# Left k/v rows on 128 partitions, and a new order of weight conversion, copies and u steps, in an attention with two MLPs

## The chip, the core and the metric

The kernel runs on one core of one Trainium2 chip. The metric is the time of one execution on the device in microseconds (us), the median of a few runs. Five engines work side by side, each through its own instructions in a fixed order: PE (TensorE: matmuls and transposes; its weight loads are shown as PEld), DVE (VectorE), ACT (ScalarE), POOL (GpSimd) and SP (SyncE, which here only issues transfers). Semaphores tie them together. PSUM is the memory PE writes to, SBUF the one that everything else lives in.

## What is computed

The reference, cut to what matters (float32, except that the five weights are float64):

```python
# attention: q, k, v (4, 8, 576, 64), phi (4, 8, 576, 32)
a = softmax(phi, axis=2)                       # over the 576 positions
k_m = einsum('bhsm,bhsd->bhmd', a, k)
v_m = einsum('bhsm,bhsd->bhmd', a, v)
attn = softmax(q @ k_m.transpose(0, 1, 3, 2) / 8)
x = (attn @ v_m), heads merged                 # (2304, 512)
# first MLP: w_a, w_b (512, 1536), w_out (1536, 512)
x = ((x @ w_a) * (x @ w_b)) @ w_out
# second MLP: w_in (512, 2048), w_out (2048, 512), elu between
out = elu(x @ w_in) @ w_out
```

## The kernel before

**Attention, lines 293 to 482 and the loop after line 530.** It runs over four batches, called b here (i in the loop). The eight heads of a batch lie as two halves u, in each of which four heads times 32 memory slots fill 128 partitions. For each batch: `a_max` (DVE), `a_exp` (ACT) and `a_end` (DVE) make the softmax of phi over the positions; `stage_aT` transposes it with PE and ACT copies it to the tile a; `stage_kv` sums k (n = 0) and v (n = 1) over the positions into pk, four times a batch, each with 16 matmuls over four blocks of 128 positions from kv_t and four over the 64 positions that are left, from left_t; `stage_m`, `stage_turn`, `stage_kT` and `stage_vT` scale and place the sums; `stage_scores` makes the scores (sc and, for the 64 positions left, sl); `stage_softmax` (DVE) takes the row maximum off, `stage_exp` (ACT) exponentiates, `stage_norm` (DVE) divides by the sums, and `stage_xT` transposes the result and splits it into xhi (ACT) and xlo (DVE). The row softmax of batch i is finished while batch i+1 runs.

**Weights.** They come as 64-bit words, a unit of 128x512 of them (512 KB) in a tile raw, of which there are three. A unit is turned into float32 parts: two ACT instructions (`magnitude` makes a, `low_word` makes lw) and seven slots of `piece`, six of them with a DVE instruction (about 3.2 us of DVE in a row). `fill(n)` does the next n slots at the place where it is called. Units are numbered in the order of use: ab(0,0), ab(0,1), ab(1,0), ab(1,1), o1(0), ab(2,0) and so on. SP loads three of them among the attention's inputs (("unit",) in the list seq, which `more_loads` works off), POOL the others, one when a conversion reaches slot 3.

**First MLP.** Since x is attn times v_m, `step_u(f, p)` multiplies a column block f of w_a and w_b with v_m of two batches into u_ps; ACT copies it to u's hi part, and a deferred DVE instruction makes the lo part. `steps_ab(f, b)` then multiplies u with xhi and xlo, two PSUM tiles (ab_ps) of 12 matmuls each, and forms a*b (a_sb, gh, gl); `steps_o1` multiplies that with w_out (o_ps). `step` sets the order inside one such step by a string: PE's work, then by ORDER "0f1a2" deferred work of kind 0, the fill, deferred work of kind 1, the evacuation a of the PSUM tile, deferred work of kind 2 (the usual kind). The list `order` sets the order of the steps. `pstile` hands out PSUM tiles in turn: two during the attention, four after it, so a tile must be read out before the second or fourth next is written. The second MLP (`step_h`, `steps_o2`) follows, with the same `step`.

Everything stands on each engine in the order in which the code records it.

Of the kernel before, what the change touches and what calls it, by code (L numbers as in the profile page):

```python
# [21 lines left out]
def attention_then_two_mlps(ctx, tc, q, kv, kv_left, phi, w_ab, w_o1, w_i2, w_o2, out):  # L22
# [15 lines left out]
    M = 32  # L38
# [34 lines left out]
    NRAW, NSHORT, NLONG = 3, 4, 4  # L73
# [19 lines left out]
    cu = {}  # L93
    ready = {}
# [52 lines left out]
    def piece():  # L147
# [70 lines left out]
    FILLS, FILLS2 = (0, 7, 7, 7), (0, 0, 0, 0)  # L218
# [59 lines left out]
    ident = p0.tile([P, P], F32, name="ident", bufs=1)  # L278

# [66 lines left out]
    def a_end(b, u):  # L346
        sm = st["sm", b, u]
        nc.vector.tensor_scalar(out=sm, in0=sm, scalar1=1e-9, scalar2=None, op0=ALU.add)
        nc.vector.reciprocal(out=sm, in_=sm)

    def stage_aT(b, us=(0, 1)):
        t = st["phi", b]
        if us[0] == 0:
            st["a", b] = p0.tile([P, 2, NJ + 1, P], F32, tag="a", name="a_t", bufs=1)
        a = st["a", b]
        tp, tl = pstile("tp_a"), pone("tl_a")
# [6 lines left out]
        nc.scalar.activation(  # L363
            out=a[:, c, 0:NJ, :].rearrange("p u j s -> p u (j s)"), in_=tp[:, c], func=AF.Copy
        )
        nc.scalar.activation(
            out=a[0:LEFT, c, NJ, :], in_=tl[0:LEFT, 0:2 * P].rearrange("p (u s) -> p u s", u=2)[:, c], func=AF.Copy
        )
        if us[-1] == 1:
            more_loads("phi")  # L370

    def stage_kv(b, n, u):
# [113 lines left out]
    def step_u(f, p, amount):  # L486
# [22 lines left out]
        step(pe, lambda: nc.scalar.activation(out=hi, in_=src, func=AF.Copy), amount)  # L509
# [3 lines left out]
    with tc.manual_schedule():  # L513
        make_identity(nc, ident)
        pair = p0.tile([P, 2, 2, P // 2], F32, name="pair", bufs=1)
# [10 lines left out]
        nc.gpsimd.memset(edge, 0.0)  # L526
        more_loads()
        for u in range(2):
            a_max(0, u)
            a_exp(0, u)  # L530
            stage_aT(0, (u,))
        for u in range(2):
            a_end(0, u)
        for i in range(B):

            for n in (1, 0):
# [339 lines left out]
```

## Time and profile before

| | |
|---|---|
| median of 3 runs | 816.09 us (814.43 to 816.77) |
| the profiled execution | 816.6 us, of which 814.8 are the span |
| PE busy, matmuls | 790.4 us (97%) |
| DVE busy | 589.4 us (72%) |
| ACT busy | 398.7 us (49%) |
| read and written in DRAM | 52.17 MB, 4.72 MB |

Busy time is that of an engine's instructions; the profile also names what ended the idle time ahead of an instruction. PEclk is the clock granted to TensorE, 1.00 being 2.4 GHz and 0.50 being 1.2 GHz. A matmul "128x288 x4" in a timeline is four in a row, with the time from the first start to the last end.

### The profile page before, as it was taken

The numbers are of one execution on the slowest core, as the hardware profiler recorded it, in microseconds if no ns is written. First come the engines' busy times: TensorE is split into PE (matmuls) and PEld (weight loads), VectorE is DVE, ScalarE is ACT, GpSimd is POOL, SyncE is SP. The second block draws the span as 40 slices with busy tenths as digits, with TensorE's granted clock in tenths as the row PEclk, the third lists the DMA queues.
The fourth block names the chain that finished last, engine by engine and source line by source line (L and its number), as shares of the span: only waits on it lengthen the run. The fifth ranks groups of instructions, "written<-read, shape, count | busy, mean of one in ns | idle before, by whom it ended". The sixth has DMA issues, their size and how long they took to land.

```text
span 814.8 us, 14254 instructions
## 1 busy us (share of the span) xinstructions
PE 790.4 (97%) x6032; PEld 728.1 (89%) x6032; DVE 589.4 (72%) x971; ACT 398.7 (49%) x616; POOL 40.3 (5%) x87
## 2 busy tenths in 40 slices
PE   5889899999999999999999999999999999999998
PEld 3778889999999999999999889988999888999896
DVE  2689797788868884677878644779777787676564
ACT  4365575534443442343468555445655456553350
POOL 2000010000000000000000000000000000000000
PEclk9899999999999999999999999999999999999999
DMA  9971032121212120011001200111111011100006
GB/s 332 363 277 53 27 109 100 52 79 57 75 52 79 55 76 27 27 53 52 1 27 53 78 1 27 51 53 52 50 53 45 35 52 42 37 0 1 1 1 232
DMA packets 16815, 57.79 MB, mean 71 GB/s; under 512 B 1776, under 2 KB 1776, under 8 KB 16752
## 3 DMA queue, kind: packets, MB, share of 16 engines
q0 software_dynamic: 9360, 34.08, 11.9%
q1 hardware_dynamic: 7392, 22.81, 7.8%
q8 instruction: 47, 0.77, 0.4%
q14 instruction: 16, 0.13, 0.1%
HBM read 52.17 MB, written 4.72 MB: 70 GB/s over the span
## 4 chain that ended last, share of the span: by engine, by line
PE 91%; DVE 4%; DMA 2%; ACT 1%; issue 1%; SPq 0%; DVEq 0%
PE o_ps L776 25%; PE h_ps L733 25%; PE o_ps L639 19%; PE ab_ps L597 18%; PE u_ps L500 2%; DMA y<-in_q_dram 2%; PE pk L383 1%; PE sc L425 1%; DMA kv_t<-in_kv_dram 1%; DVE u L510 0%; DVE y L468 0%; DVE ssm L463 0%; DVE y L452 0%; DVE smx L451 0%; DVE gl L608 0%
## 5 line engine op out<-in xcount | busy, mean ns | idle before, releaser
L597 PE MATMUL ab_ps<-xhi,u 128*128 128x288 f32 x768 | 140.4, 300 | 3.0 <-DVE u L510 3.0
L597 PEld LDWEIGHTS ab_ps<-xhi,u 128*128 128x128 f32 x768 | 115.2, 190 | 9.1 <-issue 3.5
L776 PE MATMUL o_ps<-ulh,g2h 128*128 128x512 f32 x288 | 113.7, 395 | 0.0
L776 PE MATMUL o_ps<-ull,g2h 128*128 128x512 f32 x288 | 113.6, 394 | 0.0
L776 PE MATMUL o_ps<-ulh,g2l 128*128 128x512 f32 x288 | 103.0, 395 | 0.0
L751 DVE SCALAR_TENSOR_TENSOR e<-e,th 128x768 f32<-128x768 f32 x48 | 46.0, 959 | 75.2 <-ACT e L748 74.8
L733 PE MATMUL h_ps<-yh,usl 128*128 128x384 f32 x384 | 97.8, 335 | 0.0
L733 PE MATMUL h_ps<-yl,ush 128*128 128x384 f32 x384 | 97.8, 335 | 0.0
L733 PE MATMUL h_ps<-yh,ush 128*128 128x384 f32 x384 | 97.6, 335 | 0.0
L744 ACT ACTIVATE e<-h_ps 128x768 f32<-128x768 f32 x48 | 38.9, 811 | 96.2 <-PE h_ps L733 94.0
L639 PE MATMUL o_ps<-gh,ulh 128*128 128x288 f32 x384 | 82.6, 296 | 1.8 <-DVE u L510 1.6
L597 PE MATMUL ab_ps<-xlo,u 128*128 128x288 f32 x384 | 82.7, 297 | 0.0
L639 PE MATMUL o_ps<-gh,ull 128*128 128x288 f32 x384 | 82.3, 295 | 0.0
L639 PE MATMUL o_ps<-gl,ulh 128*128 128x288 f32 x384 | 82.3, 295 | 0.0
L604 ACT ACTIVATE a_sb<-ab_ps 128x576 f32<-128x576 f32 x48 | 31.2, 651 | 84.6 <-PE ab_ps L597 84.1
L733 PEld LDWEIGHTS h_ps<-yh,ush 128*128 128x128 f32 x384 | 69.5, 188 | 1.3
L606 DVE TENSOR_TENSOR a_sb<-a_sb,ab_ps 128x576 f32<-128x576 f32 x48 | 36.1, 753 | 47.3 <-PE ab_ps L597 46.9
L733 PEld LDWEIGHTS h_ps<-yh,usl 128*128 128x128 f32 x384 | 69.4, 188 | 0.0
L733 PEld LDWEIGHTS h_ps<-yl,ush 128*128 128x128 f32 x384 | 69.3, 188 | 0.0
L776 PEld LDWEIGHTS o_ps<-ulh,g2l 128*128 128x128 f32 x288 | 54.0, 187 | 13.2
L776 PEld LDWEIGHTS o_ps<-ulh,g2h 128*128 128x128 f32 x288 | 54.0, 187 | 12.7
L776 PEld LDWEIGHTS o_ps<-ull,g2h 128*128 128x128 f32 x288 | 54.0, 187 | 12.5
(92 smaller groups left out, 1331.0 us busy)
## 6 DMA issues: line engine op xcount, KB each, us to landing
raw<-in_w_o_dram POOLq DMA_DIRECT2D x28, 512.0 KB, 3.6
raw<-in_w_ab_dram POOLq DMA_DIRECT2D x21, 512.0 KB, 3.6
kv_t<-in_kv_dram SPq DMA_DIRECT2D x16, 512.0 KB, 12.2
raw<-in_w_i_dram POOLq DMA_DIRECT2D x16, 512.0 KB, 3.5
y<-in_q_dram SPq DMA_DIRECT2D x8, 576.0 KB, 12.6
out_dram<-y SPq DMA_DIRECT2D x8, 512.0 KB, 2.9
phi_t<-in_phi_dram SPq DMA_DIRECT2D x3, 576.0 KB, 11.8
raw<-in_w_ab_dram SPq DMA_DIRECT2D x3, 512.0 KB, 12.3
```

The costliest lines, as they stand in the source:

```text
L383: nc.tensor.matmul(pk[M * h:M * h + M, D * u:D * u + D], a[0:P if j < NJ else LEFT, u, j, M * h:M * h + M], rows, start=(j == 0), stop=(j ...
L425: nc.tensor.matmul(sc[:, u, j * P:(j + 1) * P], qs[u][:, t, j * P:(j + 1) * P], kt[:, u, t * P:(t + 1) * P], start=(t == 0), stop=(t == 1))
L500: nc.tensor.matmul(ps[j:j + M, o, k * 256:k * 256 + 256], vt[r, 2 * k + c, 2 * p + o], w[r, c * 256:c * 256 + 256], start=True, stop=True, ...
L597: nc.tensor.matmul(ps[:, h, 0:HS], u[:, kk, w, n * P:n * P + P], x[b][:, kk, h * HS:(h + 1) * HS], start=(kk == 0 and i == 0), stop=(kk == ...
L604: nc.scalar.activation(out=a_sb, in_=ps[:, :, 0:HS], func=AF.Copy)
L606: nc.vector.tensor_tensor(out=a_sb, in0=a_sb, in1=ps[:, :, 0:HS], op=ALU.mult)
L639: nc.tensor.matmul(ps[:, h, 0:HS], w[:, cc], g[:, h * HS:(h + 1) * HS], start=(n == 0 and i == 0), stop=(n == len(fs) - 1 and i == 2),)
L733: nc.tensor.matmul(ps[:, h, 0:HB], w[:, c], x[:, c, h * HB:(h + 1) * HB], start=(c == 0 and i == 0), stop=(c == KC - 1 and i == 2),)
L744: nc.scalar.activation(out=e, in_=ps[:, :, 0:HB], func=AF.Relu, scale=-1.0)
L751: nc.vector.scalar_tensor_tensor(out=e, in0=e, scalar=1.0, in1=th, op0=ALU.add, op1=ALU.mult)
L776: nc.tensor.matmul(ps[:, k, :], g[:, c * P:(c + 1) * P], w, start=(f == fs[0] and i == 0), stop=(f == fs[-1] and i == 2),)
```

## The change

- **Left rows.** The 64 positions left of both halves u are loaded on 128 partitions, row 2s+u, in one tile of half the width (256 KB as before). `a_end(b, 1)` copies phi's last 64 positions interleaved into rest (DVE), one 128x128 transpose takes the place of two, and two ACT copies with a scale of 0 or 1 per partition (parity) make a_left, one for each u with the other's rows zero.
- **Conversion.** Units 0 and 1 are converted ahead of batch 0, unit 2 at the end of batch 1's transposes, unit 3 in batch 2, none in batch 3. SP loads the first seven units: one behind batch 0's phi, one behind its v, one each in batches 1 and 2, three behind the last q. POOL loads none until then. There are six ush tiles where there were four.
- **Order.** `edge` and the load of ACT's table stand at the start. In batch 3, `stage_exp(2)` stands behind both halves of `stage_m`. A u step's evacuation stands last ("012fa"). In the first MLP's list a `tick` stands ahead of `stage_norm(3)`, the fill of two ab steps (four PSUM tiles) moves to the two after `stage_xT(3)`, and u(2,1) stands behind ab(1,3).

SP, at the start, before and then of the change:

```order
L294 DMA phi_t<-in_phi_dram 128x576 x2
L303 DMA left_t<-in_kv_left_dram 64x1024
L308 DMA kv_t<-in_kv_dram 128x1024 x4
L103 DMA raw<-in_w_ab_dram 128x512
L294 DMA phi_t<-in_phi_dram 128x1152 x2
L298 DMA y_77<-in_q_dram 128x1152 x2
```

```order
L303 DMA phi_t<-in_phi_dram 128x576 x2
L104 DMA raw<-in_w_ab_dram 128x512
L312 DMA left_t<-in_kv_left_dram 128x512
L317 DMA kv_t<-in_kv_dram 128x1024 x2
L104 DMA raw<-in_w_ab_dram 128x512
L317 DMA kv_t<-in_kv_dram 128x1024 x2
L303 DMA phi_t<-in_phi_dram 128x1152 x2
L307 DMA y_77<-in_q_dram 128x1152 x2
```

The unit behind kv_t moved to behind phi, and a second one, which POOL loaded at this time, stands among the kv_t loads.

DVE in batch 1, from the end of the conversion to the row softmax of batch 1 (sc), before and then of the change; ssm and y_79 are the sums and the scores of batch 0:

```order
L182 TENSOR_TENSOR lw<-lw,p_489 128x512
L190 TENSOR_TENSOR ush<-a,lw 128x512
L463 TENSOR_REDUCE ssm<-y_79 128x32
L463 TENSOR_REDUCE ssm<-y_79 64x8
L465 TENSOR_SCALAR ssm<-ssm 128x32
L466 RECIPROCAL ssm<-ssm 128x32
L465 TENSOR_SCALAR ssm<-ssm 64x8
L466 RECIPROCAL ssm<-ssm 64x8
L468 TENSOR_TENSOR y_79<-y_79,ssm 128x1024
L468 TENSOR_TENSOR y_79<-y_79,ssm 64x256
L337 TENSOR_REDUCE nm<-phi_t 128x1 x2
L451 TENSOR_REDUCE smx<-sc 128x32
```

```order
L477 TENSOR_TENSOR y_79<-y_79,ssm 128x1024
L477 TENSOR_TENSOR y_79<-y_79,ssm 64x256
L169 TENSOR_SCALAR a<-a 128x512
L172 TENSOR_SCALAR a<-a 128x512
L177 SCALAR_TENSOR_TENSOR a<-raw,a 128x512
L183 TENSOR_SCALAR p_540<-a 128x512
L189 TENSOR_TENSOR lw<-lw,p_540 128x512
L197 TENSOR_TENSOR ush<-a,lw 128x512
L347 TENSOR_REDUCE nm<-phi_t 128x1 x2
L460 TENSOR_REDUCE smx<-sc 128x32
```

The conversion moved from ahead of `stage_norm(0)` to behind it, ahead of batch 1's row maximum.

DVE in the first MLP, around u(0,1), before and then of the change:

```order
L182 TENSOR_TENSOR lw<-lw,p_1070 128x512
L463 TENSOR_REDUCE ssm<-y_79 128x32
L463 TENSOR_REDUCE ssm<-y_79 64x8
L465 TENSOR_SCALAR ssm<-ssm 128x32
L466 RECIPROCAL ssm<-ssm 128x32
L465 TENSOR_SCALAR ssm<-ssm 64x8
L466 RECIPROCAL ssm<-ssm 64x8
L468 TENSOR_TENSOR y_79<-y_79,ssm 128x1024
L468 TENSOR_TENSOR y_79<-y_79,ssm 64x256
L190 TENSOR_TENSOR a<-a,lw 128x512
L608 TENSOR_TENSOR gl<-a_sb,gh 128x576
L510 TENSOR_TENSOR u<-u_ps,u 128x4x256
```

```order
L189 TENSOR_TENSOR lw<-lw,p_1079 128x512
L623 TENSOR_TENSOR gl<-a_sb,gh 128x576
L519 TENSOR_TENSOR u<-u_ps,u 128x4x256
L472 TENSOR_REDUCE ssm<-y_79 128x32
L472 TENSOR_REDUCE ssm<-y_79 64x8
L474 TENSOR_SCALAR ssm<-ssm 128x32
L475 RECIPROCAL ssm<-ssm 128x32
L474 TENSOR_SCALAR ssm<-ssm 64x8
L475 RECIPROCAL ssm<-ssm 64x8
L477 TENSOR_TENSOR y_79<-y_79,ssm 128x1024
L477 TENSOR_TENSOR y_79<-y_79,ssm 64x256
L621 TENSOR_TENSOR a_sb<-a_sb,ab_ps 128x576 x2
```

u's lo part moved from behind `stage_norm(3)` and a conversion step to ahead of them.

The diff, cut to its core:

```diff
-    NRAW, NSHORT, NLONG = 3, 4, 4
+    NRAW, NSHORT, NPAIR, NLONG = 3, 6, 3, 4
...
+    def ahead():
+        n = state["n"]
+        magnitude(n)
+        low_word(n)
...
-            load_unit()
+            if ("unit",) not in seq:
+                load_unit()
...
-        t = pl.tile([P, 2, 2, 2, P], F32, tag="left", name="left_t", bufs=2)
-        nc.sync.dma_start(out=t[0:LEFT], in_=kv_left[b])
+        t = pl.tile([P, 2, 2, P], F32, tag="left", name="left_t", bufs=2)
+        nc.sync.dma_start(out=t, in_=kv_left[b].rearrange("s u n c d -> (s u) n c d"))
...
-    seq = [("phi", 0, (0,)), ("phi", 0, (1,))]
+    seq += [("phi", 0, (0,)), ("phi", 0, (1,)), ("unit",)]
     for b in range(B):
-        seq += [("left", b)] + [("kv", b, n, u) for n in (1, 0) for u in range(2)]
-        seq += [("unit",)] if b < 3 else []
+        seq += [("left", b)] + [("kv", b, 1, u) for u in range(2)] + [("unit",)] * (b == 0)
+        seq += [("kv", b, 0, u) for u in range(2)] + [("unit",)] * (b in (1, 2))
...
+    seq += [("unit",)] * 3
...
+        if u == 1:
+            nc.vector.tensor_copy(out=rest, in_=st["phi", b][:, :, SM:S].rearrange("p u s -> p s u"))
...
-        for u in us:
-            nc.tensor.transpose(tl[0:LEFT, u * P:(u + 1) * P], t[:, u, SM:S], ident)
+        if us[-1] == 1:
+            tl = pone("tl_a")
+            nc.tensor.transpose(tl[:, 0:P], rest.rearrange("p s u -> p (s u)"), ident)
...
+        for u in range(2 * us[-1]):
+            nc.scalar.activation(out=a_left[:, u], in_=tl[:, 0:P], func=AF.Copy, scale=parity[:, u:u + 1])
...
-        step(pe, lambda: nc.scalar.activation(out=hi, in_=src, func=AF.Copy), amount)
+        step(pe, lambda: nc.scalar.activation(out=hi, in_=src, func=AF.Copy), amount, "012fa")
...
+        nc.gpsimd.memset(edge, 0.0)
+        nc.scalar.activation(out=edge, in_=edge, func=AF.Exp)
...
+        for u in range(2):
+            a_end(0, u)
+        ahead()
+        for u in range(2):
             stage_aT(0, (u,))
...
+        fill(7)
+        ahead()
+        fill(7)
...
-                if n and i:
+                if i and n == (i + 1 < B):
                     stage_exp(i - 1)
-            fill(FILLS[i])
...
                 stage_aT(i + 1)
+                if i:
+                    ahead()
+                    fill(7)
...
-                 ("do", lambda: stage_norm(last)), ("ab", 1, 0), ("ab", 0, 2),
-                 ("do", lambda: stage_xT(last)), ("ab", 1, 1), ("u", 1, 1), ("ab", 0, 3), ("ab", 1, 2),
-                 ("u", 2, 0), ("u", 2, 1), ("ab", 1, 3)]
+                 ("do", tick), ("do", lambda: stage_norm(last)), ("ab", 1, 0, 0), ("ab", 0, 2, 0),
+                 ("do", lambda: stage_xT(last)), ("ab", 1, 1, 2), ("u", 1, 1), ("ab", 0, 3, 2), ("ab", 1, 2),
+                 ("u", 2, 0), ("ab", 1, 3), ("u", 2, 1)]
```

## Rows read from the trace of the kernel before

**Rows 1.** The page, part 4: the chain that ended last, by engine.

```profile
PE 91%; DVE 4%; DMA 2%; ACT 1%; issue 1%; SPq 0%; DVEq 0%
```

**Rows 2.** Busy us (x instructions) of PE, PEld, DVE, ACT, POOL; PEclk, DMA share, GB/s.

```profile
130.00:200.00 70.00, 70.00 (x624) 68.20 (x623) 54.42 (x108) 33.95 (x54) 5.33 (x10) 1.00 0.23 76
200.00:300.00 100.00, 100.00 (x946) 96.41 (x945) 80.36 (x154) 43.14 (x68) 6.87 (x12) 1.00 0.19 64
```

**Rows 3.** The same columns, by stretches of the input transfers.

```profile
2.00:7.00 5.00, 1.10 (x5) 0.87 (x5) 1.75 (x4) 2.15 (x3) 3.73 (x16) 1.00 0.98 310
7.00:18.00 11.00, 7.67 (x186) 5.42 (x185) 2.05 (x6) 4.89 (x15) 0.00 (x0) 1.00 1.02 409
18.00:22.00 4.00, 3.03 (x23) 2.63 (x24) 2.98 (x8) 2.81 (x8) 0.00 (x0) 1.00 1.04 262
```

**Rows 4.** Timeline, batch 0's scores: start us, us, engine, instruction [idle before, ended by].

```profile
15.61 1.41 DVE L337 TENSOR_REDUCE nm<-phi_t 128x1 f32<-128x576 f32 x2 [6.70 <-DMA phi_t<-in_phi_dram]
...
19.18 2.02 PE L425 MATMUL sc<-y 128*128 128x128 f32 x16 [0.22 <-ACT a L113]
...
21.87 2.02 PE L425 MATMUL sc<-y 128*128 128x128 f32 x16 [0.66 <-DMA y<-in_q_dram]
...
23.82 1.09 PE L429 MATMUL sl<-y 128*64 128x128 f32 x8
```

**Rows 5.** Timeline, PE in `stage_kv` of batches 1 and 2.

```profile
30.19 0.37 PE L383 MATMUL pk<-kv_t,a_t 128*32 128x64 f32 x2 [2.82 <-issue]
...
46.34 0.55 PE L383 MATMUL pk<-kv_t,a_t 128*32 128x64 f32 x25 [1.27 <-issue]
```

**Rows 6.** Windows with the columns of rows 2, around those two stalls and in batch 3.

```profile
22.90:27.40 4.50, 4.31 (x127) 3.45 (x127) 4.22 (x9) 2.39 (x7) 0.00 (x0) 1.00 1.03 411
27.40:45.10 17.70, 14.88 (x253) 12.56 (x253) 11.46 (x26) 8.23 (x20) 0.53 (x1) 0.81 1.03 367
42.30:45.10 2.80, 2.77 (x128) 2.06 (x128) 2.70 (x7) 2.59 (x7) 0.00 (x0) 1.00 1.06 353
29.80:36.60 6.80, 6.41 (x79) 5.33 (x79) 2.88 (x6) 2.95 (x8) 0.53 (x1) 0.50 1.03 321
84.40:87.80 3.40, 3.40 (x16) 3.40 (x16) 1.66 (x4) 1.22 (x2) 0.00 (x0) 0.50 0.00 0
56.30:59.70 3.40, 3.40 (x164) 2.60 (x162) 3.33 (x6) 2.59 (x6) 0.00 (x0) 1.00 0.12 42
```

**Rows 7.** Transfers from 27.4 to 30.1 us, by queue: packets, MB, share of 16 engines.

```profile
q8 instruction: 1, 0.02, 2.5%
```

**Rows 8.** The chain in order of time: start us, us, what.

```profile
84.18 4.44 PE ab_ps L597 x20
...
89.76 3.38 PE ab_ps L597 x24
```

**Rows 9.** Who waited for whom from 60 to 130 us: us in total, times, longest.

```profile
PE ab_ps L597 <- DVE u L510: 3.0, 2, 2.7
PE o_ps L639 <- DVE u L510: 1.6, 1, 1.6
```

**Rows 10.** Timeline of DVE: `stage_norm(3)` to u(0,1)'s lo part, and ab(0,0) on PE.

```profile
66.65 0.53 PE L597 MATMUL ab_ps<-xhi,u 128*128 128x288 f32 x2
...
78.04 1.53 DVE L463 TENSOR_REDUCE ssm<-y 128x32 f32<-128x1024 f32 x2
...
81.64 0.68 DVE L190 TENSOR_TENSOR a<-a,lw 128x512 f32<-128x512 f32 x1
82.25 0.74 DVE L608 TENSOR_TENSOR gl<-a_sb,gh 128x576 fp32r<-128x576 f32 x1
82.92 1.21 DVE L510 TENSOR_TENSOR u<-u_ps,u 128x1024 fp32r<-128x1024 f32 x1
```

**Rows 11.** Timeline, a later round of u: its parts, and the next tile.

```profile
182.84 1.96 PE L500 MATMUL u_ps<-ush,vt 64*32 64x256 f32 x64
...
186.34 2.35 DVE L510 TENSOR_TENSOR u<-u_ps,u 128x1024 fp32r<-128x1024 f32 x2
```

More of the change, by code (lines that the diff above doesn't have):

```diff
@@ L93, in attention_then_two_mlps @@
     cu = {}
+    seq = []
     ready = {}
@@ L129, in to_hi @@
         key, long, _ = units[n]
-        if live[long] == (NLONG if long else NSHORT):
+        if live[long] == (NLONG if long else NPAIR):
             return False
         live[long] += 1
-        tag, nb = ("ul", NLONG) if long else ("us", NSHORT)
-        hi = conv.tile([P, 512], F32R, tag=tag + "h", name=tag + "h", bufs=nb)
-        lo = conv.tile([P, 512], F32R, tag=tag + "l", name=tag + "l", bufs=nb)
+        tag, nh, nl = ("ul", NLONG, NLONG) if long else ("us", NSHORT, NPAIR)
+        hi = conv.tile([P, 512], F32R, tag=tag + "h", name=tag + "h", bufs=nh)
+        lo = conv.tile([P, 512], F32R, tag=tag + "l", name=tag + "l", bufs=nl)
         nc.scalar.activation(out=hi, in_=cu[n]["a"].bitcast(F32), func=AF.Copy)
@@ L278, in attention_then_two_mlps @@
     ident = p0.tile([P, P], F32, name="ident", bufs=1)
+    rest = p0.tile([P, LEFT, 2], F32, name="rest", bufs=1)
+    a_left = p0.tile([P, 2, P], F32, name="a_left", bufs=1)
+    parity = p0.tile([P, 2], F32, name="parity", bufs=1)
     st = {}
@@ L353, in stage_aT @@
         if us[0] == 0:
-            st["a", b] = p0.tile([P, 2, NJ + 1, P], F32, tag="a", name="a_t", bufs=1)
+            st["a", b] = p0.tile([P, 2, NJ, P], F32, tag="a", name="a_t", bufs=1)
         a = st["a", b]
-        tp, tl = pstile("tp_a"), pone("tl_a")
+        tp = pstile("tp_a")
         for u in us:
@@ L359, in stage_aT @@
                 nc.tensor.transpose(tp[:, u, j * P:(j + 1) * P], t[:, u, j * P:(j + 1) * P], ident)
-        for u in us:
-            nc.tensor.transpose(tl[0:LEFT, u * P:(u + 1) * P], t[:, u, SM:S], ident)
+        if us[-1] == 1:
+            tl = pone("tl_a")
+            nc.tensor.transpose(tl[:, 0:P], rest.rearrange("p s u -> p (s u)"), ident)
         c = slice(us[0], us[-1] + 1)
[L363 to L368, printed above, removed]
+        nc.scalar.activation(out=a[:, c].rearrange("p u j s -> p u (j s)"), in_=tp[:, c], func=AF.Copy)
+        for u in range(2 * us[-1]):
+            nc.scalar.activation(out=a_left[:, u], in_=tl[:, 0:P], func=AF.Copy, scale=parity[:, u:u + 1])
         if us[-1] == 1:
@@ L381, in stage_kv @@
                 c, d = h // 2, slice(D * (h % 2), D * (h % 2) + D)
-                rows = t[:, j, c, d] if j < NJ else left[0:LEFT, u, n, c, d]
-                nc.tensor.matmul(pk[M * h:M * h + M, D * u:D * u + D],
-                                 a[0:P if j < NJ else LEFT, u, j, M * h:M * h + M], rows,
+                w, rows = (a[:, u, j], t[:, j, c, d]) if j < NJ else (a_left[:, u], left[:, n, c, d])
+                nc.tensor.matmul(pk[M * h:M * h + M, D * u:D * u + D], w[:, M * h:M * h + M], rows,
                                  start=(j == 0), stop=(j == NJ), tile_position=(0, M * h))
@@ L513, in attention_then_two_mlps @@
     with tc.manual_schedule():
+        nc.gpsimd.memset(edge, 0.0)
+        nc.scalar.activation(out=edge, in_=edge, func=AF.Exp)
         make_identity(nc, ident)
+        nc.vector.tensor_reduce(out=parity, in_=ident.rearrange("p (s u) -> p u s", u=2), op=ALU.add, axis=AX.X)
         pair = p0.tile([P, 2, 2, P // 2], F32, name="pair", bufs=1)
@@ L569, in attention_then_two_mlps @@
             tick()
+            if i + 1 == B:
+                ahead()
             for u in range(2 if i + 2 < B else 0):
@@ L577, in attention_then_two_mlps @@
                 a_end(i + 2, u)
-            state["ahead"] = i > 0
             if i and i + 1 < B:
                 stage_xT(i - 1)
+        state["ahead"] = True
         stage_exp(B - 1)
@@ L680, in attention_then_two_mlps @@
             elif kind == "u":
-                step_u(*args, RATE_U)
+                step_u(*args[0:2], args[2] if len(args) > 2 else RATE_U)
             else:
-                f, b = args
-                steps_ab(f, b, RATE_AB)
+                f, b = args[0:2]
+                steps_ab(f, b, args[2] if len(args) > 2 else RATE_AB)
                 for e in pend:
```

9 lines of the change are left out of this document (1 added, 8 removed).

## Prediction

> **What bounds the kernel now.** First the chain of work that ended last: PE holds 91% of it [rows 1]. Then the stretches of time: from 130 us on, PE is busy without a gap (70.00 of 70 us, 100.00 of 100) at full clock [rows 2]. What is done on PE there the change does not touch, so the time can come only from the first 125 us. In those I read three things.
>
> The input transfers keep the 16 DMA engines busy from 2 to 55 us. They move 409 GB/s from 7 to 18 us, but 310 from 2 to 7 and 262 from 18 to 22, at the same busy share [rows 3]; there are two more such dips, at 31 to 36 and 44 to 49 us. There are four, and four loads of left rows, which alone write 64 partitions.
>
> PE has done batch 0's scores at 23.82 + 1.09 = 24.91 us [rows 4] and begins ab(0,0) at 66.65 [rows 10]: 41.7 us, nearly all of it PE's own work in a row. In it are two stalls of 2.82 and 1.27 us in the middle of a run of matmuls that wait for nothing new, shown as "issue" [rows 5]. Between them PE issued 253 + 253 counted instructions, and in the 4.5 us before the first 127 + 127, in the 2.8 us before the second 128 + 128 [rows 6]. During the first a transfer of 0.02 MB on the instruction queue ran [rows 7]. I read this as PE's instructions coming in blocks of about 256, a block being asked for when the one before is begun. That makes the block take 4.5 + 2.82 = 7.3 us in the first case and 2.8 + 1.27 = 4.1 in the second, with the data queues full. In batch 3, with the DMA engines at 0.12, PE ran 164 + 162 instructions in 3.4 us with no stall [rows 6].
>
> The third thing is the first MLP's start, 66.65 to 122 us. PE waits for u's lo part on DVE, 3.0 us in two waits before ab (2.7 the longer) and 1.6 before o1 [rows 9].
>
> The granted clock stood at 0.50, which is 1.2 GHz, from 29.8 to 36.6 and from 84.4 to 87.8 us [rows 6], each time behind one of PE's two longest waits (2.82 and 2.7). In the second stretch 20 matmuls took 4.44 us where 24 take 3.38 at full clock [rows 8], so 4.44 - 3.38 x 20/24 = 1.6 us are lost. The first is twice as long and not all PE's (6.41 of 6.8 busy [rows 6]); by the same share it lost at most 3.2, and I take 2.5.
>
> **The change, part by part. A: to the end of batch 0's scores.** Ahead of batch 1's phi, SP and POOL load as many bytes as before, only in another order. What is left is the dip from 2 to 7 us: 5 x (1 - 310/409) = 1.2 us if it went wholly; part of it is the start, and I take 0.9, with ends 0 and 1.2. From that phi's landing (15.61) to the scores' first half (19.18) the chain over DVE, ACT and PE is 3.57 us [rows 4]. It gets the copy to rest: no row shows it; a DVE instruction on eight times the elements takes 1.21 [rows 10], so between 0.15 and 0.4, and I take 0.25. The second half of the scores waited for q, to 21.87; without the dip from 18 to 22, 4 x (1 - 262/409) = 1.4 us, and the 0.9, q is there at 19.6, before the first half ends. So 15.61 - 0.9 + 3.57 + 0.25 + 2 x 2.02 + 1.09 = 23.7 us for 24.91: **A = -1.2**. The load of ACT's table and the two early conversions run while ACT and DVE wait for transfers and cost nothing; if the first unit's bytes came late, ACT, which holds the copies of a behind it, would hold up v's sums, by as much as the unit's 0.5 MB takes at 409 GB/s, 1.3 us, which the wait for kv then hides again.
>
> **B: from there to ab(0,0).** PE's own work stays but for one transpose in place of two, about 0.3 us over three batches. The conversions move on DVE; PE waits for DVE nowhere here, since the sums that it transposes are a batch old; the conversion that now stands ahead of batch 1's maximum takes some of the time that DVE wins. So B is the two stalls, the slow clock, and what is new of that kind: 2.82 + 2.5 + 1.27 = 6.6 us before. The data queues stay full until about 52 us (8 us less for dips and two units fewer ahead of the last q, 4 us more for three units behind it). For a block I take the mean of 7.3 and 4.1, 5.7 us: a wait of 5.7 - 4.5 = 1.2 in batch 1 and 5.7 - 2.8 = 2.9 in batch 2; the ends are 0 to 2.8 and 1.3 to 4.5. Batch 3 comes as the queues drain: 0.5, ends 0 and 4.6 (7.3 less the 2.7 us that 256 instructions take there). A slow stretch behind the 2.9 is as likely as not: 1.0, ends 0 and 2.5. Together 5.6, so **B = 5.6 - 6.6 - 0.3 = -1.3**.
>
> **C: ab(0,0) to 122 us.** The waits were 3.0 + 1.6 and the slow stretch 1.6: 6.2 us. u(0,1)'s lo part now stands ahead of `stage_norm(3)`, which took 81.64 - 78.04 = 3.6 us of DVE [rows 10], so ab(0,2) has it in time, 0.1 us late at most. What is late next is `stage_xT(3)`: behind u(0,1), two ab's give PE 2 x 3.38 = 6.8 us [rows 8], and DVE needs some 2.0 for gl and the wait for ACT's hi part, 0.74, 1.21 and 3.6, 7.5 in all: a wait of 0.75. Then u(1,1)'s lo part: behind that norm DVE has six instructions like gl (0.74), xlo (1.5), seven conversion slots (0.68 or less, 3.7 together) and the lo part (1.21) [rows 10], 10.8 us, while PE gets from `stage_xT(3)` over ab(1,1), u(1,1) and ab(0,3) to the place in 9.7: 1.1. The wait before o1, with u(2,1) behind it, I put at 0.5 of 1.6. That leaves 2.5, ends 0.5 and 5: **C = 2.5 - 6.2 = -3.7**.
>
> **D: the later rounds.** The u step's new order comes nine more times. In one, the two u's end on PE at 184.80 and their lo parts on DVE at 188.69 [rows 11], with PE not waiting. ACT's hi copy moves behind a gh copy, and DVE's lo parts move together with it; PE's gapless stretch covers that, and I cost it at 0. If the cover were gone, each round would cost up to the 1.6 us that PE once waited for such a part [rows 9].
>
> **The sum.** -1.2 - 1.3 - 3.7 = -6.2: 816.6 - 6.2 = 810.4 us for the profiled execution. The median of the runs lies 0.5 us below that execution, so I forecast 809.9 us.
>
> **Rivals.** First, the instruction blocks stop mattering: PE's stalls were waits for data after all, or a block comes in 4 us and less. Then B is -6.6 - 0.3 = -6.9 and the sum -11.8: 804.3 us. For it speaks that one block of the two came in 4.1; against it that both stalls stand 506 counted instructions apart and in mid-run. The Trainium skill (Runtime: NRT & Kernel Launch, Instruction fetch mechanics) says that instructions come in blocks of 256 through a queue of their own, and that crossing a block is mostly hidden. By that rule this rival would be the forecast; [rows 5, 7] show the size of the block but not the hiding.
>
> Second, the change doesn't do what it says: left rows on 128 partitions are no faster, the dips stay. Then A is 0.25 in place of -1.2, B and C as above: 811.9 us. The rows only show that dips and left loads are equal in number. The Trainium skill (SBUF — State Buffer, Door 1: The DMA port swizzle) says that partitions 0 to 63 reach half of the ports, which fits and makes this rival unlikely.
>
> Third, slower: the instruction blocks again, from the other side. PE now gets to its dense runs of 256 instructions in 2.7 us while the data queues are still full. If each block takes 7.3 us there, batches 1 to 3 wait 2.8, 4.5 and 4.6 us, each with a slow stretch of 2.5 behind it: 19.4 for 6.6, B = 12.5, and the sum 7.6: 823.7 us. Without batch 3 it is 12.3 for 6.6 and the sum is 0.5, no change. So this decides if waits and slow clock in batches 1 to 3 pass 6.6 + 0.3 + 4.9 = 11.8 us.
>
> **How the numbers follow.** The forecast (807 to 812.5) 0.50, the first rival 0.22, the second 0.10, the third in full 0.06, its half without batch 3 (813 to 817) 0.12. The range reaches over the first rival to 803 us and up to 814.5, which leaves out the third and part of its half. A measurement here can tell about 0.3%, 2.4 us, from no change: faster is below 813.6. The forecast, both first rivals and a quarter of the half make faster 0.85; the rest of the half makes same 0.09; slower 0.06.
>
> **What would show it.** A: no stretch below 380 GB/s from 7 to 50 us, and batch 0's sl ends before 24 us. B: "issue" stalls of PE in `stage_kv` of 0 to 2.8 us in batch 1 and 1.3 to 4.5 in batch 2, ab(0,0) starting at 62 to 66 us. C: no wait above 1.5 us for u's lo part, and no stretch at 0.50 behind ab(0,0). D: PE gapless behind 125 us. The forecast is wrong if PE waits in the later rounds, if the dips stay, or if a stall in `stage_kv` grows past 4.5 us.

## The result, and the profile of the changed kernel

The changed kernel takes 807.11 us, the median of four runs (806.99 to 808.01), for 816.13 before (four runs as well). The ratio is 0.9895, 95% interval 0.9878 to 0.9912: faster, by 9.0 us where 6.2 were forecast. Its profiled execution took 807.16 us with a span of 805.4. Cut at the prediction's places (starts and ends of rows in the two timelines; C ends with the first weight load of the first o1 behind which PE has no gap, at 129.35 before and 122.01 now, and D in the last tile of the first MLP's last o1, at 406.73 and 396.70):

| stretch, us | before | changed | difference | forecast |
|---|---|---|---|---|
| A: to the end of batch 0's scores | 24.91 | 24.36 | -0.55 | -1.2 |
| B: to ab(0,0) | 41.74 | 38.96 | -2.78 | -1.3 |
| C: to the first gapless o1 | 62.70 | 58.69 | -4.01 | -3.7 |
| D: into the first MLP's last o1 | 277.38 | 274.69 | -2.69 | 0 |
| rest, to the end of the span | 408.08 | 408.69 | +0.61 | 0 |

First the chain by engine, as in [rows 1]. PE still holds nearly all of it:

```profile
PE 90%; DVE 3%; ACT 2%; issue 1%; DVEq 0%; ACTq 0%
```

The windows of [rows 3] (PE, PEld, DVE, ACT, POOL busy, granted clock, DMA share, GB/s):

```profile
2.00:7.00 5.00, 1.76 (x9) 1.75 (x9) 2.26 (x7) 1.85 (x6) 3.13 (x15) 1.00 0.89 302
7.00:18.00 11.00, 7.42 (x180) 5.89 (x179) 7.88 (x16) 6.18 (x15) 0.00 (x0) 1.00 1.02 414
18.00:22.00 4.00, 3.73 (x31) 3.48 (x30) 1.77 (x5) 3.54 (x11) 0.00 (x0) 1.00 1.03 408
```

The dip from 18 to 22 us is gone (408 GB/s for 262); the one from 2 to 7 has stayed (302 for 310). So left rows on 64 partitions did not make that one; what does, these rows don't show. The timeline of batch 0's scores, to set beside [rows 4]:

```profile
15.22 0.69 DVE L197 TENSOR_TENSOR ush<-a,lw 128x512 f32<-128x512 f32 x1
...
15.88 1.41 DVE L347 TENSOR_REDUCE nm<-phi_t 128x1 f32<-128x576 f32 x2
...
19.53 3.81 PE L434 MATMUL sc<-y 128*128 128x128 f32 x32 [0.27 <-DMA y<-in_q_dram]
...
23.27 1.09 PE L438 MATMUL sl<-y 128*64 128x128 f32 x8
```

Batch 1's maximum (nm) starts 0.27 us later than before, and with no wait for phi that shows: DVE comes to it from the second unit's conversion (ush). The scores now run in one piece.

The timeline's rows of PE with an "issue" wait, for [rows 5], and the window behind the last of them, for [rows 6]:

```profile
27.24 0.32 PE L393 MATMUL pk<-left_t,a_left 128*32 128x64 f32 x8 [1.14 <-issue]
...
40.03 0.48 PE L393 MATMUL pk<-kv_t,a_t 128*32 128x64 f32 x19 [1.04 <-issue]
...
54.42 0.25 PE L393 MATMUL pk<-kv_t,a_t 128*32 128x64 f32 x2 [3.35 <-issue]
```

```profile
56.60:60.00 3.40, 3.40 (x37) 2.59 (x22) 3.33 (x8) 2.73 (x7) 0.00 (x0) 0.56 0.00 0
```

Three stalls for two, 5.5 us for 4.1. The granted clock falls once, to the lower of its two levels (1.2 GHz) for most of this window, behind the longest stall: batch 3's u takes 1.80 us for 1.09, and its scores 4.67 for 3.7, so 1.7 us are lost, where the prediction took 2.5 for before. Stalls and slow clock together have grown, by 0.6 us, and yet B has shrunk by 2.78. The next rows say why: stage_kv's matmuls on PE, one tile after the other (start, us), first before, then now:

```profile
24.84 0.65 PE L383 MATMUL pk<-kv_t,a_t 128*32 128x64 f32 x32
25.42 0.32 PE L383 MATMUL pk<-left_t,a_t 64*32 64x64 f32 x8
25.67 0.65 PE L383 MATMUL pk<-kv_t,a_t 128*32 128x64 f32 x32
```

```profile
24.29 0.65 PE L393 MATMUL pk<-kv_t,a_t 128*32 128x64 f32 x32
24.76 0.29 PE L393 MATMUL pk<-left_t,a_left 128*32 128x64 f32 x8
24.87 0.63 PE L393 MATMUL pk<-kv_t,a_t 128*32 128x64 f32 x32
```

A group of 40 takes 25.67 - 24.84 = 0.83 us before and 24.87 - 24.29 = 0.58 now. Twelve groups lie in B: 12 x 0.25 = 3.0 us. The shape changed from 64 to 128 rows in the left matmuls alone.

Who waits for whom from 60 to 130 us, for [rows 9]:

```profile
PE ab_ps L612 <- DVE u L519: 1.0, 1, 1.0
...
PE o_ps L654 <- DVE u L519: 0.9, 1, 0.9
...
PE tp_x L485 <- DVE y L477: 0.4, 1, 0.4
```

These are 2.3 us where the prediction had 2.5, and no stretch of slow clock follows them.

Last, two neighbouring steps of the later rounds in the chain in order of time (start, us, what), before and now:

```profile
305.25 9.59 PE ab_ps L597 x72
314.84 9.60 PE o_ps L639 x72
```

```profile
296.17 9.36 PE ab_ps L612 x72
305.53 9.52 PE o_ps L654 x72
```

The same 72 matmuls, without a gap and at full clock in both, take 1 to 2% less. This adds up to D, and nothing in the prediction accounts for it.

### The profile page after: what moved, and what is told of

It is laid out like the page before. It is cut to its first block, busy times and chain, and to the rows that moved or that the text cites. A ratio compares the mean times of both kernels' runs of the same rounds, so it can differ in the third digit from the quotient of the medians.

```text
span 805.4 us, 14253 instructions
## 1 busy us (share of the span) xinstructions
PE 782.9 (97%) x6028; PEld 723.1 (90%) x6028; DVE 590.7 (73%) x976; ACT 399.7 (50%) x620; POOL 38.3 (5%) x83
## 3 DMA queue, kind: packets, MB, share of 16 engines
q1 hardware_dynamic: 8224, 24.91, 7.9%
## 4 chain that ended last, share of the span: by engine, by line
PE 90%; DVE 3%; ACT 2%; issue 1%; DVEq 0%; ACTq 0%
PE o_ps L791 25%; PE h_ps L748 25%; PE o_ps L654 18%; PE ab_ps L612 17%; PE u_ps L509 3%; PE sc L434 1%; DVE gl L623 0%; DVE u L519 0%; PE tp_x L485 0%; PE pk L393 0%; DVE a L177 0%; ACT xhi L69 0%; DVE a_sb L621 0%; PE sl L438 0%; ACT u L518 0%
## 5 line engine op out<-in xcount | busy, mean ns | idle before, releaser
L612 PE MATMUL ab_ps<-xhi,u 128*128 128x288 f32 x768 | 138.3, 296 | 1.0 <-DVE u L519 1.0
L612 PEld LDWEIGHTS ab_ps<-xhi,u 128*128 128x128 f32 x768 | 113.2, 188 | 7.3 <-ACT gh L622 2.5
```

What stands on the lines that cost most here:

```text
L612: nc.tensor.matmul(ps[:, h, 0:HS], u[:, kk, w, n * P:n * P + P], x[b][:, kk, h * HS:(h + 1) * HS], start=(kk == 0 and i == 0), stop=(kk == ...
```

## The experiments

Each kernel is the one before or the changed one with one edit. A to D are cut as above; times are medians. The ratio is to the kernel before on the same chip, whose own runs spread from 812 to 819 us over all these.

| kernel | us | ratio, 95% interval | A | B | C | D |
|---|---|---|---|---|---|---|
| before | 816.13 | | 24.9 | 41.7 | 62.7 | 277.38 |
| changed | 807.11 | 0.9878 to 0.9912 | 24.4 | 39.0 | 58.7 | 274.69 |
| before, left rows alone | 812.16 | 0.9942 to 0.9973 | 25.8 | 40.9 | 61.6 | 274.69 |
| before, 64 rows filled to 128 | 815.57 | 0.9982 to 1.0013 | 26.4 | 41.7 | 61.8 | 277.39 |
| before, MLP order alone | 813.31 | 0.9959 to 0.9991 | 27.9 | 40.4 | 58.7 | 277.38 |
| before, left rows and MLP order | 808.92 | 0.9877 to 0.9925 | 26.2 | 40.9 | 58.7 | 274.69 |
| before, two tiles elsewhere | 812.93 | 0.9946 to 0.9983 | 27.9 | 38.6 | 62.0 | 274.69 |
| changed, gh and gl 32 bytes off | 810.08 | 0.9906 to 0.9945 | 26.1 | 38.1 | 58.7 | 277.14 |
| changed, a_sb 32 bytes off | 807.50 | 0.9865 to 0.9907 | 23.7 | 39.3 | 58.7 | 274.69 |
| changed, 128 instructions ahead | 805.98 | 0.9857 to 0.9920 | 25.3 | 37.5 | 58.7 | 274.69 |
| changed, 84 ahead, gh 64 off | 806.87 | 0.9868 to 0.9905 | 24.3 | 36.9 | 58.7 | 276.92 |
| changed, late loads | 805.76 | 0.9853 to 0.9898 | 25.6 | 38.0 | 58.7 | 274.69 |
| changed, all together, xhi 64 off | 806.88 | 0.9858 to 0.9901 | 24.7 | 38.9 | 58.6 | 275.53 |
| changed, 84 ahead alone | 804.91 | 0.9847 to 0.9892 | 25.8 | 35.5 | 58.7 | 274.69 |

D repeats to 0.01 us wherever gh and gl lie at the same place modulo 128 bytes (xhi and xlo too), and C to 0.1 us in all kernels with the first MLP's new order. With the old order C is 61.6 to 62.7, and the kernel before has the longest. A and B do not repeat: kernels that are the same up to that point differ by 3 us in one profiled execution, by where stalls and slow stretches fall.

### The left rows

The first kernel makes the change to the left rows alone, in the kernel before (load, the copy to rest, one transpose, the masked copies):

```diff
-        nc.sync.dma_start(out=t[0:LEFT], in_=kv_left[b])
+        nc.sync.dma_start(out=t, in_=kv_left[b].rearrange("s u n c d -> (s u) n c d"))
...
-                rows = t[:, j, c, d] if j < NJ else left[0:LEFT, u, n, c, d]
+                w, rows = (a[:, u, j], t[:, j, c, d]) if j < NJ else (a_left[:, u], left[:, n, c, d])
```

> The kernel before with the left rows on 128 partitions alone. Theory (each change of a matmul between 64 and 128 rows costs PE about 0.12 us, two to a group of 40): a group of 40 in stage_kv goes from 0.83 to 0.58 us, 12 groups on the path give 3.0 us; the transposes 0.5; the dips in GB/s are gone and give up to 0.6 in batch 0; and gh stands where it stands in the changed kernel, so o1's matmuls take 132.2 for 133.3 ns, 1.2 us. With stalls as before 811 us, and 809 to 814 with stalls of another size. Rival (the left rows matter only to the transfers): groups stay at 0.83 us, and the time is 815.

It took 812.16 us, with groups of 0.58 us in its timeline, as the theory had it. The windows at three of the former dips (the columns as above):

```profile
18.00:22.00 4.00, 3.78 (x19) 3.54 (x20) 2.73 (x9) 3.85 (x11) 0.00 (x0) 0.59 1.02 403
31.00:36.00 5.00, 4.80 (x40) 4.28 (x39) 4.76 (x11) 1.42 (x3) 0.53 (x1) 1.00 1.02 407
44.00:48.00 4.00, 3.85 (x33) 3.28 (x34) 2.60 (x6) 3.94 (x10) 0.53 (x1) 0.75 1.03 407
```

The second keeps the load on 64 partitions and fills the other 64 with zeros once, so that the left matmuls read 128 rows:

```diff
+        for t in lefts:
+            nc.gpsimd.memset(t[LEFT:P], 0.0)
+        nc.gpsimd.memset(a_one[LEFT:P, :, NJ], 0.0)
...
-                rows = t[:, j, c, d] if j < NJ else left[0:LEFT, u, n, c, d]
+                rows = t[:, j, c, d] if j < NJ else left[:, u, n, c, d]
```

> The kernel before with its left load on 64 partitions as it was, but with the other 64 partitions of the left rows and of their a filled with zeros once, so that every matmul of stage_kv reads 128 rows. Theory (PE pays for each change between 64 and 128 rows): a group of 40 goes from 0.83 to 0.58 us, while the four dips in GB/s stay; 12 groups give 3.0 us, less what the blocks of instructions take back because PE gets to them sooner: 811 to 816 us. Rival (the layout of the load makes the matmuls faster): the group stays at 0.83 us, 816.

Its timeline of stage_kv, and its windows:

```profile
26.35 0.65 PE L385 MATMUL pk<-kv_t,a_one 128*32 128x64 f32 x32
26.82 0.29 PE L385 MATMUL pk<-left,a_one 128*32 128x64 f32 x8
26.93 0.63 PE L385 MATMUL pk<-kv_t,a_one 128*32 128x64 f32 x32
```

```profile
18.00:22.00 4.00, 3.47 (x19) 3.00 (x20) 2.60 (x8) 3.64 (x11) 0.00 (x0) 0.73 1.04 273
32.00:36.00 4.00, 2.68 (x22) 2.55 (x23) 3.76 (x11) 0.82 (x2) 0.53 (x1) 1.00 1.05 230
44.00:48.00 4.00, 4.00 (x60) 3.35 (x51) 1.83 (x4) 3.08 (x9) 0.00 (x0) 0.60 1.05 278
```

The two effects come apart: the group is at 0.58 us with the load as it was, and the dips are there with the matmuls as in the changed kernel. So 64 rows among 128 cost PE 0.25 us in a group of 40, and loading on 64 partitions costs the stream a third of its rate and more in these windows. (It is not the longer rows of that load: kv_t's have the same 1024 words on 128 partitions, and the stretch of [rows 3] in which they come ran at 409 GB/s.) The Trainium skill (SBUF — State Buffer, Door 1: The DMA port swizzle) has it that partitions 0 to 63 reach half of the ports; these windows agree, with 230 to 278 GB/s against 403 to 407. In time this kernel gained nothing (815.57): PE is through stage_kv sooner, and then waits for kv (1.1 us), for q (1.6) and 3.8 us for its instructions. With both effects, in the first kernel, PE waits 3.8 us for its instructions too and begins ab(0,0) at 66.66 us, where it was 66.65 before. Of the 3.6 us by which that kernel is faster than the one before on the same chip (812.16 for 815.71), 2.7 are D, which is no work of the left rows (below): the kernel that has this D alone, with two tiles elsewhere, takes 812.93. So what PE saves in stage_kv it mostly loses again in waits, and the left rows by themselves brought some 0.8 us by the medians, within the two intervals.

### The first MLP

The list, the amounts and the u step's order, in the kernel before:

```diff
-        step(pe, lambda: nc.scalar.activation(out=hi, in_=src, func=AF.Copy), amount)
+        step(pe, lambda: nc.scalar.activation(out=hi, in_=src, func=AF.Copy), amount, "012fa")
...
-                 ("do", lambda: stage_norm(last)), ("ab", 1, 0), ("ab", 0, 2),
+                 ("do", tick), ("do", lambda: stage_norm(last)), ("ab", 1, 0, 0), ("ab", 0, 2, 0),
```

> The kernel before with the first MLP's new order alone (the list, the amounts and the u step's order). Theory: ab(0,0) to the first gapless o1 takes 58.7 us in place of 62.7, and the stretch behind it stays at 277.4: 812.1 us. Rival (the gain in the later rounds is the u step's order): the later stretch falls to 274.7 as well, 809.4 us. Second rival (the order gains only with the conversions made ahead): the first stretch stays above 61 us and the time above 814.5.

C is 58.68 us, the changed kernel's to 0.01, and its waits are the same:

```profile
PE ab_ps L597 <- DVE u L510: 1.0, 1, 1.0
PE o_ps L639 <- DVE u L510: 0.9, 1, 0.9
...
PE tp_x L476 <- DVE y L468: 0.4, 1, 0.4
```

So C's gain comes from this part, without conversions made ahead. It is 4.0 us against the profile before, and 2.9 to 3.3 against the other three kernels with the old order. D stays at 277.38: the u step's order, which stands in each later round, does nothing there. The time fell by 2.4 us and not by 4, because PE came to ab(0,0) 1.7 us later in this kernel's profiled execution (A 3.0 us longer, B 1.4 shorter); the granted clock was 0.56 from 18 to 24 us. A was longer in the same way in the kernel with two tiles elsewhere, whose batch 0 is also the one of before.

The last kernel of this kind has both parts and leaves conversions, unit loads, the table load and batch 3's `stage_exp(2)` as they were:

> The kernel before with the left rows on 128 partitions and the first MLP's new order, but with the conversions, the unit loads and the early load of ACT's table where they were. Theory (these cost nothing and bring nothing): first MLP to the first gapless o1 58.7 us, later rounds 274.7, and up to ab(0,0) 62.5 to 66.5 by how the stalls and the slow stretches fall: 806 to 810 us. Rival (the conversions made ahead carry part of the gain): the first MLP over 60 us, or ab(0,0) behind 66.7: 811 us and more.

808.92 us, with C and D as expected but ab(0,0) at 67.1, later than expected, so that neither theory is met in full. Stalls of 3.2 and 1.3 us and two stretches at 0.50 lie ahead of it:

```profile
18.00:22.00 4.00, 3.64 (x17) 3.60 (x18) 2.58 (x10) 4.00 (x12) 0.00 (x0) 0.50 1.03 406
44.00:48.00 4.00, 4.00 (x47) 3.50 (x40) 2.02 (x5) 3.26 (x9) 0.07 (x1) 0.50 1.04 412
```

The changed kernel is 1.8 us faster, but the two intervals overlap almost wholly. What the conversions, the loads and `stage_exp(2)` in their new order bring stays open between nothing and some 2 us.

### The later rounds

The changed kernel needs other tiles in p0: rest 512 bytes a partition, a_left 1024, parity 32 with its rounding, and a_t 1024 less, 544 more in all. The tiles of the first MLP under it (a_sb, gh, gl) stand 544 bytes lower: gh begins at byte 142432 of a partition in the built kernel before, which is 96 beyond a multiple of 128, and at 141888 in the changed one, 64 beyond. conv is 2048 bytes larger, so xhi, xlo and u stand 2048 higher. The first test moves gh to 64 beyond, with a gap of 32 bytes, and xhi to the changed kernel's place:

```diff
+    vt = pa.tile([P, KC, B, M], F32, name="vt")
     xhi = [pa.tile([P, 2, S], F32R, name=f"xhi{b}") for b in range(B)]
...
-    vt = pa.tile([P, KC, B, M], F32, name="vt")
+    p0.tile([P, 8], F32, name="gap", bufs=1)
     ident = p0.tile([P, P], F32, name="ident", bufs=1)
```

> The kernel before with two tiles elsewhere and nothing else: 32 bytes of gap ahead of ident, which puts gh at the same place modulo 256 bytes as in the changed kernel, and vt ahead of xhi, which moves xhi and xlo by 2048 bytes to the changed kernel's addresses. Theory (what a matmul takes depends on where its operands lie in SBUF): o1's mean from one matmul to the next falls from 133.3 to 132.2 ns, ab's from 134.1 to something else, and the stretch from the first gapless o1 to the last falls from 277.4 to 275 to 276.5 us: 814 to 815 us. Rival (the changed kernel's gain there comes from the order of the u step or of the conversions): 277.4 and 816.1 us.

Not a single instruction differs, and D is 274.69 us:

```profile
293.16 9.51 PE o_ps L640 x72
302.68 9.36 PE ab_ps L598 x72
```

The kernel with the left rows alone has the same D; there gh is moved and xhi is not. So it is gh's side and not xhi's. The other way round, 32 bytes more in the changed kernel:

```diff
+    p0.tile([P, 8], F32, name="gap", bufs=1)
     ident = p0.tile([P, P], F32, name="ident", bufs=1)
```

> The changed kernel with an unused tile of 32 bytes a partition ahead of ident, which moves gh, gl and a_sb by 32 bytes and nothing else that the first MLP uses. Theory (the 2.69 us of the later rounds come from these tiles' place: they stand at a multiple of 64 bytes in the changed kernel and in the two runs that had the gain too, 32 bytes off in the kernel before): the stretch from the first gapless o1 to the last goes back from 274.69 to 277.4 us, 809.8 us. Rival (the gain hangs on something else that those runs share): 274.7 us, and 807.1.

```profile
298.64 9.59 PE ab_ps L613 x72
308.23 9.60 PE o_ps L655 x72
```

Nearly all is lost again, D 277.14. Then a_sb alone, with the 32 bytes between it and gh:

```diff
+            if (f, b) == (0, 0):
+                pb.tile([P, 8], F32, tag="gap", name="gap", bufs=1)
             gh = pb.tile([P, S], F32R, tag="gh", name="gh", bufs=9)
```

> The changed kernel with an unused tile of 32 bytes between a_sb and gh, which moves a_sb by 32 bytes and leaves gh and gl in place. Theory (the place of gh and gl, which matmuls read, sets the 2.7 us of the later rounds): 274.7 us there, 807.1 in all. Rival (the place of a_sb, which only ACT and DVE touch, does it, through what they take from PE's reads): 276.5 to 277.4 us, 809 to 810.

D 274.69, so a_sb's place does nothing and that of gh or gl, or of both, does it. I had taken the rule to be multiples of 64 bytes. The run with gh at a multiple of 128 (below) shows that it is not: D is 276.92 there, with 9.58 and 9.57 us for the two steps. Of the four places modulo 128 that ran (0, 32, 64, 96) only 64 is fast, at both addresses that had it. In all of these xhi and xlo stood at a multiple of 128. With gh left at 64 and xhi and xlo moved to 64 as well (also below) D was 275.53, so whether gh's place counts by itself or against theirs stays open. Matmuls of ab, which don't read gh, gain as well as those of o1, which do; what on the chip ties the two together these runs do not show.

### The blocks of instructions

From here on PE's instructions are counted from the start: weight loads, matmuls (the 253 + 253 of [rows 6]) and the semaphore instructions among them. So counted, the three stalls of the changed kernel stand one behind 705, 1217 and 1729, which are 512 apart. The first kernel has thirty-two small matmuls at the head, four counted instructions each, while PE waits for phi anyway:

```diff
         more_loads()
+        warm = pone("warm")
+        for _ in range(32):
+            nc.tensor.matmul(warm[0:M, 0:D], ident[:, 0:M], ident[:, 0:D], start=True, stop=True, tile_position=(0, 0))
```

> The changed kernel with 32 small matmuls more (128 counted PE instructions) at the head, while PE waits for phi. Theory (a block of 512 counted instructions, asked for 256 before its first, with the answer 3 to 5.5 us away): the stalls stand at counted instructions 705, 1217 and 1729 whatever stands there, so each block now begins 128 instructions earlier in the program, in the second or third load of a stage_kv, and the 256 ahead of it hold the scores. PE then has no issue stall over 0.3 us in batches 1 to 3 and no stretch at 0.50: 1.14 + 1.04 + 3.34 + 1.6 = 7.1 us less than the changed kernel, 800 us. Rival (PE waits for data or at a fixed place of the program): the three stalls stand where they stood, at the same size, and the time is 807.

The three stalls are gone from their places, so they hang on the count and not on data. But one stands elsewhere (PE rows with a wait, 24 to 60 us):

```profile
31.65 1.94 PE L371 MATMUL tp_a<-ident,phi_t 128*128 128x128 f32 x8 [2.35 <-issue]
...
43.79 0.45 PE L414 MATMUL pt<-pair,m 128*64 128x64 f32 x8 [1.30 <-DVE sm L358]
...
56.98 1.10 PE L509 MATMUL u_ps<-ush,vt 64*32 64x256 f32 x32 [1.27 <-DVE xlo L70]
```

It stands two behind counted instruction 961, halfway between 705 and 1217. Blocks are 256 long, as the prediction had them, and not 512, as this run's expectation had. A bound costs time where PE is through the 256 ahead of it before the block comes: in stage_kv of the changed kernel PE takes about 2 us for them, and here, partly outside it, 3.4, while the block came after 5.8. With this stall, the slow clock behind it (0.56 from 31.6 to 35 us) and DVE late next (sm, xlo), the 7.1 us came to 1.1.

Twenty-one of them put each bound where the scores lie in the 256 ahead. This kernel also has a gap of 64 bytes, which puts gh at a multiple of 128:

> The changed kernel with 21 small matmuls more (84 counted instructions) at the head, and a gap of 64 bytes ahead of ident, which puts gh at a multiple of 128 bytes. Theory (blocks of 256 counted instructions, the next asked for when one begins): none of the blocks' bounds in batches 1 to 3 now has all its 256 ahead of it in stage_kv, so no issue stall passes 1.5 us; what is late next is DVE, which is busy 9.7 us of 10 from 40 to 60 us, and ab(0,0) begins at 61 to 63. The place modulo 128 does nothing: 274.7 us in the later rounds. 804 to 806.5 us. Rival (blocks of 512): stalls at counted instructions 705, 1217 and 1729 alone. Second rival (128 bytes count too): later rounds of 273 us or less.

ab(0,0) begins at 61.2, with one stall of 1.16 us, but D is 2.2 us longer, for 806.87 us in all. The same without the gap:

> The changed kernel with the 84 counted instructions at the head alone, and gh, gl and a_sb left where the changed kernel has them. Theory (the terms add up: the later rounds hang on the place of these tiles, ab(0,0)'s start on the blocks' bounds): 274.69 us in the later rounds where the run with the 64-byte gap had 276.92; ab(0,0) begins at 61 to 62.5 us, with no issue stall over 1.3; 803.5 to 805.5 us, faster than both kernels. Rival (what the blocks give is taken back by waits for kv or by a stretch at 0.50, as in the run that put all edits together): ab(0,0) at 63 or later, 806 to 807.5 us.

```profile
41.04 0.45 PE L414 MATMUL pt<-pair,m 128*64 128x64 f32 x8 [1.08 <-DVE sm L358]
...
52.12 0.26 PE L393 MATMUL pk<-kv_t,a_t 128*32 128x64 f32 x3 [1.01 <-issue]
...
55.53 1.10 PE L509 MATMUL u_ps<-ush,vt 64*32 64x256 f32 x32 [1.28 <-ACT vt L425]
```

804.91 us, D back at 274.69, and ab(0,0) at 61.3: below both kernels. Against the changed kernel the intervals still overlap a little (the ratio to before is 0.9870 for 0.9895).

The changed kernel with the last three unit loads behind batch 3's first copy of m, on POOL:

```diff
-    seq += [("unit",)] * 3
...
+                if n and i + 1 == B:
+                    nc.gpsimd.tensor_copy(out=edge[:, 0:1], in_=st["m", n, i][:, 0, 0:1])
+                    for _ in range(3):
+                        load_unit()
```

> The changed kernel with the last three weight units loaded later, by POOL behind the copy of batch 3's first half of m, so that the data queues run empty some 4 us sooner. Theory (the block waits behind data in the queues): in batch 3 the block is there 2.8 us after it is asked for, not 5.4; the stall of 3.34 us falls under 1.0 at the same counted instruction, no stretch at 0.50 follows, and what is late next is DVE with xlo: ab(0,0) begins at 60 to 61.5 us, 804 to 805.5 us. Rival (a block takes as long with empty queues): a stall of 3 us or more at the same place, 807.

```profile
30.54 0.32 PE L392 MATMUL pk<-left_t,a_left 128*32 128x64 f32 x8 [2.80 <-issue]
...
43.88 0.48 PE L392 MATMUL pk<-kv_t,a_t 128*32 128x64 f32 x19 [1.04 <-issue]
...
56.27 0.25 PE L392 MATMUL pk<-kv_t,a_t 128*32 128x64 f32 x2 [0.60 <-issue]
```

In batch 3 it did what was expected: 0.60 us for 3.35 at the same counted instruction, 2.7 us from the first of the 256 ahead (53.6) to the block's, where the changed kernel took 5.4; and no slow clock behind it. DMA was busy 0.05 of the time from 52.2 to 56.2 us. But batch 1, which this edit does not touch, stalled 2.80 us in this execution for 1.14, with the granted clock at 0.55 from 30.5 to 34 us behind it, and ab(0,0) came at 63.6, not at 60 to 61.5. The same place took 0.0 us in the kernel with gh 32 bytes off and 0.9 in the one with a_sb moved: what a block takes with full queues differs between kernels that are alike up to there.

All of it together, with xhi and xlo 64 bytes further:

> The changed kernel with 84 counted instructions more at the head, the last three weight units loaded late by POOL, gh left where the changed kernel has it, and xhi and xlo moved by 64 bytes (u by 128). Theory: ab(0,0) begins at 60.5 to 62 us with no issue stall over 1.2 us, as with the two edits apart; in the later rounds the matmuls of ab whose moving operand starts at a multiple of 256 bytes take 1 ns more than the others in the changed kernel, so with xhi at 64 off they may gain that, and the later rounds take 272.5 to 274.7 us. 801 to 803.5 us. Rival (the place of xhi does nothing or costs): 274.7 us or more, 803 and above.

806.88 us, no gain. PE came to batch 1's kv ahead of the transfers (waits of 0.94, 0.41 and 0.61 us), a slow stretch followed (granted clock 0.57 from 28 to 32 us), and D took 0.84 us more.

## Why the prediction was right, and where it was not

**C** was right in mechanism and size: -4.0 for -3.7, the waits 0.4, 1.0 and 0.9 us where the sum had 0.75, 1.1 and 0.5, plus 0.1 that did not come. The order alone repeats the 58.7 us to 0.01. The 4.0 are helped by luck: the kernel before has the longest C of the four with the old order (61.6 to 62.7).

**A** had the wrong cause for most of its gain. The dip from 2 to 7 us did not go, so the step "15.61 - 0.9" failed (the maximum started at 15.88), and the copy to rest cost nothing that shows (0.21 us on DVE). Of 1.2 us, 0.55 came, from q: its second half kept PE waiting 0.66 us before and not at all now, against 0.27 for its first. The sign "sl ends before 24 us" was missed, at 24.36. A profile of one execution says little here: over the kernels with before's batch 0 (before, MLP order, tiles elsewhere) A is 24.9, 27.9 and 27.9, over those with the changed one and nothing ahead of it 24.4, 26.1, 25.6 and 23.7.

**B** was right in sign, -2.8 for -1.3, by two errors against each other. The step that failed is "PE's own work stays but for one transpose in place of two": it took the matmuls of stage_kv for unchanged, since their number is, and missed that a row of before already shows 64 rows among 128 at 0.25 us for 8 matmuls where 32 of the others take 0.58. That term is -3.0. Of the stalls, batch 1 came as forecast (1.14 for 1.2), batch 2 shorter (1.04 for 2.9, under the stated 1.3 to 4.5) and batch 3 longer (3.35 for 0.5): the step "batch 3 comes as the queues drain" failed, because the three unit loads moved behind the last q kept the queues full until 53 us, 2 us after PE was through the block ahead. The late-load kernel shows that with empty queues it is 0.6. The reading of the blocks itself (256 counted, asked for when the one before begins) held.

**D** was forecast at 0 because the u step's order was the only edit seen there; that edit is worth 0. What the prediction left out is that a tile's size in one pool moves the tiles of another. These 2.7 us lie outside every case that was weighed.

**The rivals.** That the dips would stay is refuted for those ahead of which left rows are loaded (408 GB/s from 18 to 22 us, 401 to 413 from 28 to 52). Its 811.9 us is the profiled execution's; the median's by the same sum is 811.4. That blocks would stop mattering is refuted: there are 5.5 us of stalls that go by the count. The Trainium skill (Runtime: NRT & Kernel Launch, Instruction fetch mechanics) has the crossing of a block mostly hidden. Of six bounds between 22 and 55 us in the changed kernel three cost nothing, and three 1.04 to 3.35 us, where PE was through the 256 ahead in 2 to 4 us. The kernel with 84 instructions ahead has one stall of 1.0 us left and is some 2 us faster than the changed one, far from the further 5.6 us that lay between forecast and rival: DVE and ACT are late next. The slower rival did not come: stalls and slow clock took 5.5 + 1.7 = 7.2 us in batches 1 to 3, where it needed more than 11.8. So the sum was 3 us too small, of which D is 2.7, and B's two errors nearly cover what A lacked and the 0.6 us of the rest. The time lay in the range by the range's width: 807.11 stands at the lower edge of the forecast's 807 to 812.5, and none of the weighed cases has the errors that led there.

## What to carry to other kernels

Matmuls on 64 rows among others on 128 cost PE time, and loads on 64 partitions slow the whole stream; here waits took back most of what filling both saved. Where tiles of a pool change size, compare the pace of the untouched matmuls elsewhere, since a move of 32 bytes alone was worth 2.5 us here. And a stall without a wait in a dense run of small instructions is read by counting instructions from the start: it is mended by putting the bound where the 256 ahead take longer, or by keeping the data queues short there.

## What the runs showed of the hardware that was not expected

- 40 matmuls of 64 columns take 0.58 us if all read 128 rows, 0.83 if 8 of them read 64.
- 72 matmuls of 288 columns take 9.52 us (o1) and 9.36 (ab behind o1) with gh and gl 64 bytes beyond a multiple of 128, 9.57 to 9.60 and 9.58 to 9.59 at 0, 32 and 96 beyond; ab behind u takes 9.78 or 9.79 in both kernels.
- One block of 256 counted PE instructions, from the first of the 256 ahead to its own first, took 2.7 us with empty data queues and 3.1 to 7.5 with full ones, and between kernels alike up to there the same bound stalled 0.0 to 2.8 us.
- The rest in the first table, 0.6 us more in the changed kernel, lies behind the last store of the output, which lands 2.0 us after its issue in both. In these last microseconds the changed kernel moves one packet of 0.01 MB on an instruction queue (q14) and the kernel before none; that it is the cause was not tested.
